# Delta-rule attention and hash-routed experts on one core: products of the experts in one of five widths, chosen by a branch of TensorE

## The chip, the core and the metric

One core of a Trainium2 chip runs the whole kernel. The metric is the device time of one execution in microseconds (us); less is better. The engines are named as in the profile: PE (TensorE: matmuls, with PEld for its weight loads), DVE (VectorE), ACT (ScalarE), POOL (GpSimd) and SP (SyncE). Each engine has a sequencer of its own that reads the engine's instructions in order.

## What is computed

The reference runs a delta-rule attention and hands its output, row by row, to a layer of eight experts:

```
# q, k, v: (4, 8, 768, 48), beta: (4, 8, 768)
k_n = k / (|k| + 1e-6)
for t in range(768):                       # per batch and head, state (48, 48)
    y[t]  = q[t] @ state
    state = state + beta[t] * outer(k_n[t], v[t] - state.T @ k_n[t])
x = y as rows (batch, t) of all heads: (3072, 384)
expert = token_ids * 2654435761 % 8        # the low three bits of the id
for e in range(8):
    rows      = x[expert == e]
    out[rows] = relu(rows @ w1[e]) @ w2[e] # w1: (8, 384, 1024), w2: (8, 1024, 384)
```

All numbers are float32. How many rows an expert gets depends on the token ids. With the inputs given here the eight experts get 364, 389, 385, 423, 360, 376, 420 and 355 of the 3072 rows.

## The kernel before

The kernel has two parts. The first (to line 827, the first 270 us or so) is the attention: time is cut into 24 chunks of 32 steps, the states stay in PSUM, and a list written out by hand orders the work of all engines (the schedule is manual: each engine executes its instructions in the order in which the program issues them). It leaves its rows in a scratch tensor in DRAM, `x_scratch`. In its last chunks, `routing()` works out on DVE, from the token ids, a table of slots: `gx` holds for each slot the row of `x_scratch` to fetch, `gidx` the row of the output to write. `routing()` is cut into steps by `yield`; the number behind a `yield` is the time that a small planner (`Work`) reckons for the step, and the chunk loop takes as many steps as it has time for.

Each expert has room for `CAP` = 424 rows, as `KT` = 4 tiles of `TS` = 106 rows. Rows beyond that go to an overflow loop at the end (line 937 on), which runs no time with these inputs. For expert 0 alone, the first three tiles (`KE`) are fetched before the attention has ended, and so hold only rows of its first 21 chunks (`CE`); `shift` moves the ranks of the later rows up so that they begin in the fourth tile. The kernel before does that for all eight experts.

The second part runs the experts one after the other. For expert e the loop has four steps:

- gemm1 (line 851): for each of the 8 blocks `fo` of 128 hidden units, 3 matmuls of 128x128 weights by 128x424 rows into one of two PSUM banks, by turns; after an even block ACT, after an odd one DVE applies the relu and copies to `h_sb`.
- rows of the expert before out (`put_all`, lines 872 to 877): for each of 4 tiles, 3 transposes by PE, a copy to `o_sb` by DVE or ACT, and an indirect DMA by POOL that scatters 112 rows.
- rows of the next expert in (`turn_one`, lines 843 and 845): for each of 4 tiles, 3 transposes by PE and a copy to `xT` by DVE.
- gemm2 (line 864): for each of the 3 blocks `co` of 128 outputs, 8 matmuls into one of two banks, then a copy to `yT` by ACT or DVE (line 866).

A float32 matmul is two records in the profile, each with a weight load of its own, so each product of an expert has 48 records of PE and 48 of PEld. Weights sit in three sets of buffers. SP issues the loads of expert e + 3 (`load_w`, lines 83 and 86) behind gemm2 of expert e; POOL issues the gathers of expert e + 2's rows behind gemm1 of expert e.

Of the kernel before, what the change touches and what calls it, by code (L numbers as in the profile page):

```python
# [9 lines left out]
F32 = mybir.dt.float32  # L10
BF16 = mybir.dt.bfloat16
I32 = mybir.dt.int32
ACT = mybir.ActivationFunctionType
ALU = mybir.AluOpType
# [5 lines left out]
def kernel(  # L20
# [11 lines left out]
    nc = tc.nc  # L32
    P = 128
    B, H, S, D = q.shape
    N, DIN = out.shape
    E, _, F = moe_w1.shape
    C = 32
    CO = DIN // P
    FO = F // P
    NTC = N // P  # L40
# [2 lines left out]

    KT = 4
    KE = 3
    TS = 106
    TD = 112
    CAP = KT * TS  # L50
    CE = 21
    NOV = -(-(N - CAP) // P)
    NHI = E * KT + NOV
    BIG = 1 << 20


    x_dram = nc.dram_tensor("x_scratch", (N, DIN), F32, kind="Internal").ap()
# [8 lines left out]
    gidx = keep.tile([P, NHI], I32)  # L66
    gx = keep.tile([P, NHI], I32)
    ov_i = keep.tile([P, NOV + 1], I32)


    wts = ctx.enter_context(tc.tile_pool(name="wts", bufs=1))
# [39 lines left out]
    def bank(pool, tag):  # L111
        return pool.tile([P, BANK], F32, tag=tag, name="ps" + tag.upper())

    ctx.enter_context(tc.manual_schedule())
    with ExitStack() as phase1:
# [101 lines left out]
        def routing():  # L217

            V = nc.vector
# [10 lines left out]
            for b in range(B):  # L230
# [57 lines left out]
            V.tensor_tensor(sums, incl_f, sums, op=ALU.subtract)  # L288
            V.tensor_tensor(rank_f, rank_f, sums, op=ALU.add)

            yield 0.7
            shift = rt.tile([P, E], F32)
            V.tensor_scalar(out=shift, in0=incl[:, :, CE - 1], scalar1=-1.0,
                            scalar2=float(KE * TS), op0=ALU.mult, op1=ALU.add)
            V.tensor_scalar(out=shift, in0=shift, scalar1=0.0, scalar2=None, op0=ALU.max)
            V.tensor_tensor(rank[:, :, CE:], rank[:, :, CE:],
                            shift[:, :, None].to_broadcast([P, E, NTC - CE]), op=ALU.add)

            yield 0.9
            V.tensor_tensor(shift, shift, incl[:, :, NTC - 1], op=ALU.add)  # L300
            more = rt.tile([P, E, NTC], F32)
            V.tensor_tensor(more, shift[:, :, None].to_broadcast([P, E, NTC]),
                            thr[:, None, :].to_broadcast([P, E, NTC]), op=ALU.is_gt)
            blocks = rt.tile([P, E], F32)
            V.tensor_reduce(blocks, more, axis=AX.X, op=ALU.add)
# [523 lines left out]
    with tc.tile_pool(name="m_xg", bufs=8) as m_xg, \  # L829
         tc.tile_pool(name="m_h", bufs=2) as m_h, \  # L830
         tc.tile_pool(name="m_y", bufs=1) as m_y, \
         tc.tile_pool(name="m_o", bufs=5) as m_o:

        xTs = [t[:, :CO * CAP].rearrange("p (c n) -> p c n", c=CO) for t in XTs]

        yTs = [m_y.tile([P, CO, CAP + TD - TS], F32, name=f"yT{i}") for i in range(2)]
        for t in yTs:
            nc.vector.memset(t[:, :, CAP:], 0.0)

        def turn(xg, xT, col, width):  # L840
            xT_ps = bank(ps_t, "t")[:, :CO * P].rearrange("p (c n) -> p c n", c=CO)
            for co in range(CO):
                nc.tensor.transpose(xT_ps[:, co, :width], xg[:width, co * P:(co + 1) * P],
                                    ident[:width, :width])
            nc.vector.tensor_copy(xT[:, :, col:col + width], xT_ps[:, :, :width])  # L845

        def gemm1(i, xT, h_sb, cols):
            for fo in range(FO):
                h_ps = bank(*((ps_k, "k"), (ps_w, "w"))[fo % 2])
                for co in range(CO):  # L850
                    nc.tensor.matmul(h_ps[:, cols], lhsT=W1s[i][:, co, fo * P:(fo + 1) * P],  # L851
                                     rhs=xT[:, co, cols], start=(co == 0), stop=(co == CO - 1))
                if fo % 2 == 0:
                    nc.scalar.activation(h_sb[:, fo, cols], h_ps[:, cols], ACT.Relu)  # L854
                else:
                    nc.vector.tensor_scalar(out=h_sb[:, fo, cols], in0=h_ps[:, cols], scalar1=0.0,  # L856
                                            scalar2=None, op0=ALU.max)

        def gemm2(i, h_sb, yT, width):

            for co in range(CO):
                y_ps = bank(ps_s, f"s{co % 2}")
                for fo in range(FO):
                    nc.tensor.matmul(y_ps[:, :width], lhsT=W2w[i][:, fo, co * P:(co + 1) * P],  # L864
                                     rhs=h_sb[:, fo, :width], start=(fo == 0), stop=(fo == FO - 1))
                (nc.vector.tensor_copy if co % 2 else nc.scalar.copy)(yT[:, co, :width],  # L866
                                                                      y_ps[:, :width])

        def put(yT, col, width, idx, kt, alone):
            o_ps = bank(*((ps_g, "g"), (ps_y, "y"))[kt % 2])  # L870
            for co in range(CO):
                nc.tensor.transpose(o_ps[:width, co * P:(co + 1) * P], yT[:, co, col:col + width],
                                    ident)
            o_sb = m_o.tile([P, DIN], F32, name="o_sb")
            (nc.scalar.copy if kt % 2 else nc.vector.tensor_copy)(o_sb[:width],  # L875
                                                                  o_ps[:width, :DIN])
            scat = nc.gpsimd.indirect_dma_start(  # L877
                out=out[:, :], out_offset=bass.IndirectOffsetOnAxis(ap=idx[:width], axis=0),
                in_=o_sb[:width], in_offset=None, bounds_check=N - 1, oob_is_err=False)
            if alone:  # L880
                tc.declare_no_dep(scat.ins, group="scatters", reason="disjoint rows")
                tc.add_to_no_dep_group("scatters", scat.ins)

        xgs = {(0, kt): xg0[kt] for kt in range(KT)}

        def fetch(e):
            for kt in range(KT):
                xgs[e, kt] = m_xg.tile([P, DIN], F32, name="xg")
                gather(x_dram, gx[:, e * KT + kt:e * KT + kt + 1], xgs[e, kt])

        def turn_one(e, kt):
            turn(xgs.pop((e, kt)), xTs[e % 3], kt * TS, TS)

        def put_all(e):
            for kt in range(KT):
                put(yTs[e % 2], kt * TS, TD, gidx[:, e * KT + kt:e * KT + kt + 1], kt, True)

        def new_h():
            return m_h.tile([P, FO, CAP], F32, name="h_sb")


        gather(x_dram, gx[:, KE:KT], xg0[KE])
        for kt in range(KE):
            turn_one(0, kt)
        for _ in load_w(1, nc.gpsimd):
            pass

        for i in range(8):
            nc.vector.memset(m_xg.tile([P, DIN], F32, name="xg"), 0.0)
        fetch(1)  # L910
        for _ in load_w(2, nc.gpsimd):
            pass
        for e in range(E):
            h_sb = new_h()
            if e == 0:
                gemm1(0, xTs[0], h_sb, slice(0, KE * TS))
                turn_one(0, KE)
                gemm1(0, xTs[0], h_sb, slice(KE * TS, CAP))
            else:
                gemm1(e % 3, xTs[e % 3], h_sb, slice(0, CAP))  # L920
            if e + 2 < E:
                fetch(e + 2)
            if e > 0:

                put_all(e - 1)
            if e + 1 < E:
                for kt in range(KT):
                    turn_one(e + 1, kt)
            gemm2(e % 3, h_sb, yTs[e % 2], CAP)
            if e + 3 < E:  # L930
                for _ in load_w(e + 3, nc.sync):
                    pass
        put_all(E - 1)


        n_ov = nc.values_load(ov_i[0:1, NOV:NOV + 1], min_val=0, max_val=NOV)
        with tc.For_i(0, n_ov, 1) as it:
            ex = nc.values_load(ov_i[0:1, bass.ds(it, 1)], engines=[mybir.EngineType.Pool],
                                min_val=0, max_val=E - 1)
            for _ in load_w(None, nc.gpsimd, 0, ex):  # L940
                pass
            idx = m_o.tile([P, 1], I32, name="idx")
            nc.vector.tensor_copy(idx, gidx[:, bass.ds(it + E * KT, 1)])
            idx_x = m_o.tile([P, 1], I32, name="idx_x")
            nc.vector.tensor_copy(idx_x, gx[:, bass.ds(it + E * KT, 1)])
            xg = m_xg.tile([P, DIN], F32, name="xg")
            nc.vector.memset(xg, 0.0)
            nc.gpsimd.indirect_dma_start(
                out=xg, out_offset=None, in_=x_dram[:, :],
                in_offset=bass.IndirectOffsetOnAxis(ap=idx_x[:, 0:1], axis=0),  # L950
                bounds_check=N - 1, oob_is_err=False)
            turn(xg, xTs[0], 0, P)
            h_sb = new_h()
            gemm1(0, xTs[0], h_sb, slice(0, P))
            gemm2(0, h_sb, yTs[0], P)
            put(yTs[0], 0, P, idx[:, 0:1], 0, False)


# [26 lines left out]
```

## Time and profile before

| what | us |
|---|---|
| three runs | 595.12, 595.18, 597.61 |
| median | 595.18 |
| the profiled execution | 593.35 |
| its span, from the first to the last instruction | 591.8 |
| PE busy / weight loads busy | 527.1 / 377.6 |
| DVE / ACT / POOL busy | 271.0 / 197.5 / 255.2 |
| mean clock granted to PE | 0.944 |

The time of an execution is its span and some 1.5 us around it. Matmuls are pipelined, and their ends are modelled: the mean duration of one matmul (519 ns) overlaps the next, and the distance from start to start is read from the busy time of many. Weight loads overlap matmuls. "Issue" as the releaser of a wait means that the profile shows nothing that the engine waited for. A sequencer's own instructions (register moves, branches, waits that stand alone) are not on the page; where they are spoken of below, they are read from the trace's raw records, as is the start of a single instruction fetch. Times of such records are given from the start of the span, too.

### The profile page before, as it was taken

How to read it: one execution, taken by the hardware profiler on the slowest of the kernel's cores; microseconds unless marked ns; L12 is line 12 of the kernel's file. 1: busy time of each engine (PE TensorE's matmuls, PEld its weight loads, DVE VectorE, ACT ScalarE, POOL GpSimd, SP SyncE). 2: the span in 40 equal slices, each digit the busy share in tenths (PEclk: the TensorE clock that was granted, in tenths of full speed). 3: DMA queues.
4: the chain of work that ended last, by engine and by line, in shares of the span. 5: the costliest groups of instructions: out<-in, count | busy, mean ns of one | idle time of the engine just before them, and what ended most of it. 6: DMA issues, size and time to landing. Idle time of an engine off the chain costs nothing. (4 is left out here: it accounts for less than half of the span.)

```text
span 591.8 us, 13888 instructions
## 1 busy us (share of the span) xinstructions
PE 527.1 (89%) x5548; PEld 377.6 (64%) x5548; DVE 271.0 (46%) x717; ACT 197.5 (33%) x429; POOL 255.2 (43%) x409
## 2 busy tenths in 40 slices
PE   8968889889888577879899999999999999999991
PEld 7857878888888577766755555555555555555551
DVE  6899898989899875833210201212012030120100
ACT  5866677787786232421101111011010110110100
POOL 9509677787878764943830310503205010020112
PEclk9559899999999987986999999999999999999997
DMA  6927678698685754853973440434315300010011
GB/s 110 180 41 120 112 131 155 122 156 155 120 151 105 128 119 88 174 129 91 371 230 106 156 130 14 176 106 144 115 39 188 106 22 17 0 40 0 8 37 39
DMA packets 130242, 65.57 MB, mean 111 GB/s; under 512 B 112858, under 2 KB 120114, under 8 KB 130176
## 3 DMA queue, kind: packets, MB, share of 16 engines
q1 hardware_dynamic: 113328, 33.12, 27.1%
q0 software_dynamic: 15328, 28.39, 19.4%
q10 hardware_dynamic: 1520, 3.15, 1.8%
q8 instruction: 45, 0.74, 0.6%
q14 instruction: 21, 0.17, 0.1%
HBM read 49.67 MB, written 10.22 MB: 101 GB/s over the span
## 5 line engine op out<-in xcount | busy, mean ns | idle before, releaser
L864 PE MATMUL psS<-h_sb,w 128*128 128x424 f32 x384 | 138.1, 519 | 0.0
L877 POOL DMA_INDIRECT out_dram<-o_sb,gidx x32 | 30.4, 950 | 231.4 <-DVE o_sb L875 224.1
L864 PEld LDWEIGHTS psS<-h_sb,w 128*128 128x128 f32 x384 | 72.3, 190 | 61.0 <-issue 61.0
L856 DVE TENSOR_SCALAR h_sb<-psW 128x424 f32<-128x424 f32 (+2 forms) x36 | 19.8, 550 | 157.8 <-PE psW L851 155.1
L851 PE MATMUL psK<-xT,w 128*128 128x424 f32 (+2 forms) x216 | 76.5, 491 | 1.4 <-DVE xT L845 1.4
L851 PE MATMUL psW<-xT,w 128*128 128x424 f32 (+2 forms) x216 | 74.8, 482 | 0.0
L172 POOL DMA_DIRECT2D K<-in_k_dram x96 | 55.4, 583 | 42.6 <-PE psS L606 36.2
L517 DVE TENSOR_TENSOR U<-U,tmp 128x31 f32<-128x31 f32 (+15 forms) x186 | 63.8, 343 | 6.4
L515 DVE TENSOR_TENSOR tmp<-U,Ni 128x31 f32<-128x31 f32 (+15 forms) x186 | 63.3, 340 | 5.3
L851 PEld LDWEIGHTS psK<-xT,w 128*128 128x128 f32 x216 | 40.2, 194 | 31.9 <-issue 29.4
L851 PEld LDWEIGHTS psW<-xT,w 128*128 128x128 f32 x216 | 39.6, 191 | 29.9 <-issue 28.2
L551 POOL DMA_DIRECT2D MB<-MT x96 | 55.3, 583 | 4.5 <-PE psG L617 2.0
L178 POOL DMA_DIRECT2D V<-in_v_dram x96 | 55.3, 583 | 4.0 <-DMA V<-in_v_dram 1.3
L866 ACT COPY yT<-psS 128x424 f32<-128x424 f32 x16 | 8.2, 512 | 143.3 <-PE psS L864 115.2
L854 ACT ACTIVATE h_sb<-psK 128x424 f32<-128x424 f32 (+2 forms) x36 | 17.4, 484 | 110.3 <-PE psK L851 109.2
L452 PE MATMUL psG<-sd,w 96*64 96x64 f32 x640 | 30.0, 243 | 17.1 <-ACT sd L431 11.7
L594 PE MATMUL psW<-R,TB 128*64 128x48 f32 x736 | 33.6, 230 | 12.6 <-DVE R L579 8.3
L866 DVE COPY yT<-psS 128x424 f32<-128x424 f32 x8 | 4.8, 601 | 87.1 <-PE psS L864 87.1
L600 ACT ACTIVATE W<-psW 64x192 f32<-64x192 f32 x96 | 31.1, 324 | 39.7 <-PE psW L594 34.2
L606 PE MATMUL psS<-W,K 128*96 128x96 f32 x368 | 42.2, 260 | 1.6 <-ACT W L600 1.6
L439 ACT ACTIVATE w<-psT,own 96x512 f32<-96x512 f32 x66 | 43.2, 688 | 0.4
L606 PEld LDWEIGHTS psS<-W,K 128*96 128x96 f32 x368 | 37.4, 172 | 3.3 <-ACT W L600 1.9
(186 smaller groups left out, 696.7 us busy)
## 6 DMA issues: line engine op xcount, KB each, us to landing
w<-in_moe_w_dram SPq DMA_DIRECT2D x15, 512.0 KB
w<-in_moe_w_dram SPq DMA_DIRECT2D x20, 384.0 KB
Kd<-in_k_dram SPq DMA_DIRECT2D x24, 192.0 KB
Qd<-in_q_dram SPq DMA_DIRECT2D x24, 192.0 KB
K<-in_k_dram POOLq DMA_DIRECT2D x96, 48.0 KB
V<-in_v_dram POOLq DMA_DIRECT2D x96, 48.0 KB
x_scratch<-x_sb SPq DMA_DIRECT2D x96, 48.0 KB
TB<-TU SPq DMA_DIRECT2D x96, 32.0 KB
```

Source lines behind the costliest of these rows:

```text
L172: nc.gpsimd.dma_start(out=K4s[c % 3][quarter(i), :, i % 2, :], in_=k_r[i, c * C:(c + 1) * C])
L178: nc.gpsimd.dma_start(out=Vs[c][quarter(i)], in_=v_r[i, c * C:(c + 1) * C])
L439: nc.scalar.activation(to[:, :, :, r], psT, ACT.Copy, scale=own[:, r:r + 1])
L515: V.tensor_tensor(tmp, U[:, j:j + 1, 0:n].to_broadcast([P, m, n]), Ni[:, j, j + 1:, None].to_broadcast([P, m, n]), op=ALU.mult)
L517: V.tensor_tensor(U[:, j + 1:, 0:n], U[:, j + 1:, 0:n], tmp, op=ALU.add)
L551: eng.dma_start(out=dst[quarter(i), :, i, :], in_=src[quarter(i)])
L594: nc.tensor.matmul(psW[pair(p), i], lhsT=TBs[c % 2][:, HT * h + i, 2 * p:2 * p + 2].rearrange("k r t -> k (r t)"), rhs=Rs[h][:, i], start= ...
L600: nc.scalar.activation(Ws[h][pair(p), :, p], psW[pair(p)], ACT.Copy)
L606: nc.tensor.matmul(psS[h][:, i], lhsT=K4s[c % 3][:, HT * h + i], rhs=Ws[h][:, i], start=(c == 0 and i == 0), stop=True, skip_group_check=True)
L851: nc.tensor.matmul(h_ps[:, cols], lhsT=W1s[i][:, co, fo * P:(fo + 1) * P], rhs=xT[:, co, cols], start=(co == 0), stop=(co == CO - 1))
L864: nc.tensor.matmul(y_ps[:, :width], lhsT=W2w[i][:, fo, co * P:(co + 1) * P], rhs=h_sb[:, fo, :width], start=(fo == 0), stop=(fo == FO - 1))
L877: scat = nc.gpsimd.indirect_dma_start(out=out[:, :], out_offset=bass.IndirectOffsetOnAxis(ap=idx[:width], axis=0), in_=o_sb[:width], in_of ...
```

## The change

The routing also counts, for each expert, which of five widths holds its rows: 360, 376, 392, 408 or 424 (`WIDTHS`, from 0 to 4), and stores that number in `wid_i`. The ranks are shifted for expert 0 only. With these inputs the rows used are 375 (364 and a shift of 11), 389, 385, 423, 360, 376, 420 and 355, so the widths are 376, 392, 392, 424, 360, 376, 424 and 360.

PE's sequencer loads the number into a register (`arm`), and every group of matmuls is written five times, once per width, as the five bodies of a switch that only PE takes part in. A gemm1 group is now a pair of blocks `fo` (6 matmuls, 12 records of PE and 12 of PEld), a gemm2 group one block `co` (8 matmuls, 16 and 16 records). The switch is a jump through a register: two register moves and a product give the distance, each body starts at the beginning of a 16 KB block of instructions, holds at its top a hint that names the block behind the switch, and ends in a jump to it. Four PSUM banks instead of two serve each product, and both copies of a pair come after the pair. ACT and DVE copy all 424 columns as before. Expert 0's gemm1 has fixed widths (318, then 106 columns) and no switch; its gemm2 has one.

Between the products, the tiles of rows out and rows in alternate (out 0, in 0, out 1, in 1 and so on), and the copies of the rows in alternate between ACT and DVE.

```diff
+    WIDTHS = [CAP - 16 * i for i in range(4, -1, -1)]
...
+    wid_i = keep.tile([P, E], I32)
...
-            yield 0.7
-            shift = rt.tile([P, E], F32)
-            V.tensor_scalar(out=shift, in0=incl[:, :, CE - 1], scalar1=-1.0,
+            yield 0.9
+            shift = rt.tile([P, 1], F32)
+            V.tensor_scalar(out=shift, in0=incl[:, 0, CE - 1:CE], scalar1=-1.0,
                             scalar2=float(KE * TS), op0=ALU.mult, op1=ALU.add)
             V.tensor_scalar(out=shift, in0=shift, scalar1=0.0, scalar2=None, op0=ALU.max)
-            V.tensor_tensor(rank[:, :, CE:], rank[:, :, CE:],
-                            shift[:, :, None].to_broadcast([P, E, NTC - CE]), op=ALU.add)
-
-            yield 0.9
-            V.tensor_tensor(shift, shift, incl[:, :, NTC - 1], op=ALU.add)
+            V.tensor_scalar(out=rank[:, 0, CE:], in0=rank[:, 0, CE:], scalar1=shift[:, 0:1],
+                            scalar2=None, op0=ALU.add)
+            used = rt.tile([P, E], F32)
+            V.tensor_copy(used, incl[:, :, NTC - 1])
+            V.tensor_tensor(used[:, 0:1], used[:, 0:1], shift, op=ALU.add)
+
+            yield 1.0
+            wid = rt.tile([P, E], F32)
+            V.tensor_scalar(out=wid, in0=used, scalar1=float(WIDTHS[0]), scalar2=None,
+                            op0=ALU.is_gt)
+            for n in WIDTHS[1:-1]:
+                V.scalar_tensor_tensor(out=wid, in0=used, scalar=float(n), in1=wid, op0=ALU.is_gt,
+                                       op1=ALU.add)
+            V.tensor_copy(wid_i, wid)
+
+            yield 0.7
...
-        def turn(xg, xT, col, width):
+        def copy(eng, out, in_):
+            (nc.scalar.copy if eng is nc.scalar else nc.vector.tensor_copy)(out, in_)
+
+        def turn(xg, xT, col, width, eng):
...
-            nc.vector.tensor_copy(xT[:, :, col:col + width], xT_ps[:, :, :width])
+            copy(eng, xT[:, :, col:col + width], xT_ps[:, :, :width])
...
+        banks = [bank(*t) for t in ((ps_k, "k"), (ps_w, "w"), (ps_s, "s0"), (ps_s, "s1"))]
+
+        def widths(arm):
+
+            if isinstance(arm, int):
+                yield arm
+            else:
+                for i in tc.Switch({mybir.EngineType.PE: arm}, len(WIDTHS)):
+                    yield WIDTHS[i]
+
+        def gemm1(i, xT, h_sb, arm, lo=0, hi=CAP):
+
+            for f in range(0, FO, 2):
+                h_ps = banks[f // 2 % 2 * 2:][:2]
+                for width in widths(arm):
+                    for fo in range(2):
+                        for co in range(CO):
+                            nc.tensor.matmul(
+                                h_ps[fo][:, lo:width],
+                                lhsT=W1s[i][:, co, (f + fo) * P:(f + fo + 1) * P],
+                                rhs=xT[:, co, lo:width], start=(co == 0), stop=(co == CO - 1))
+                nc.scalar.activation(h_sb[:, f, lo:hi], h_ps[0][:, lo:hi], ACT.Relu)
+                nc.vector.tensor_scalar(out=h_sb[:, f + 1, lo:hi], in0=h_ps[1][:, lo:hi],
+                                        scalar1=0.0, scalar2=None, op0=ALU.max)
+
+        def gemm2(i, h_sb, yT, arm, hi=CAP):
 
             for co in range(CO):
...
+                y_ps = banks[co]
+                for width in widths(arm):
+                    for fo in range(FO):
+                        nc.tensor.matmul(y_ps[:, :width],
+                                         lhsT=W2w[i][:, fo, co * P:(co + 1) * P],
+                                         rhs=h_sb[:, fo, :width], start=(fo == 0),
+                                         stop=(fo == FO - 1))
+                copy((nc.scalar, nc.vector)[co % 2], yT[:, co, :hi], y_ps[:, :hi])
...
         def turn_one(e, kt):
-            turn(xgs.pop((e, kt)), xTs[e % 3], kt * TS, TS)
...
+            turn(xgs.pop((e, kt)), xTs[e % 3], kt * TS, TS, (nc.scalar, nc.vector)[kt % 2])
+
+        def put_one(e, kt):
+            put(yTs[e % 2], kt * TS, TD, gidx[:, e * KT + kt:e * KT + kt + 1], kt, True,
+                (nc.vector, nc.scalar)[kt % 2])
+
+        def arm(e):
+            return nc.values_load(wid_i[0:1, e:e + 1], engines=[mybir.EngineType.PE], min_val=0,
+                                  max_val=len(WIDTHS) - 1)
...
+        arms = {}
         for e in range(E):
             h_sb = new_h()
             if e == 0:
-                gemm1(0, xTs[0], h_sb, slice(0, KE * TS))
+                gemm1(0, xTs[0], h_sb, KE * TS, 0, KE * TS)
+                arms[0] = arm(0)
                 turn_one(0, KE)
-                gemm1(0, xTs[0], h_sb, slice(KE * TS, CAP))
+                gemm1(0, xTs[0], h_sb, CAP, KE * TS)
             else:
-                gemm1(e % 3, xTs[e % 3], h_sb, slice(0, CAP))
+                gemm1(e % 3, xTs[e % 3], h_sb, arms[e])
+            if e + 1 < E:
+                arms[e + 1] = arm(e + 1)
             if e + 2 < E:
                 fetch(e + 2)
-            if e > 0:
-
-                put_all(e - 1)
-            if e + 1 < E:
-                for kt in range(KT):
+
+            for kt in range(KT):
+                if e > 0:
+                    put_one(e - 1, kt)
+                if e + 1 < E:
                     turn_one(e + 1, kt)
-            gemm2(e % 3, h_sb, yTs[e % 2], CAP)
+            gemm2(e % 3, h_sb, yTs[e % 2], arms[e])
```

More of the change, by code (lines that the diff above doesn't have):

```diff
@@ L289, in routing @@
             V.tensor_tensor(rank_f, rank_f, sums, op=ALU.add)
-            yield 0.7
-            shift = rt.tile([P, E], F32)
-            V.tensor_scalar(out=shift, in0=incl[:, :, CE - 1], scalar1=-1.0,
+            yield 0.9
+            shift = rt.tile([P, 1], F32)
+            V.tensor_scalar(out=shift, in0=incl[:, 0, CE - 1:CE], scalar1=-1.0,
                             scalar2=float(KE * TS), op0=ALU.mult, op1=ALU.add)
             V.tensor_scalar(out=shift, in0=shift, scalar1=0.0, scalar2=None, op0=ALU.max)
-            V.tensor_tensor(rank[:, :, CE:], rank[:, :, CE:],
-                            shift[:, :, None].to_broadcast([P, E, NTC - CE]), op=ALU.add)
-            yield 0.9
-            V.tensor_tensor(shift, shift, incl[:, :, NTC - 1], op=ALU.add)
+            V.tensor_scalar(out=rank[:, 0, CE:], in0=rank[:, 0, CE:], scalar1=shift[:, 0:1],
[12 more added lines that the diff above has]
+            yield 0.7
             more = rt.tile([P, E, NTC], F32)
-            V.tensor_tensor(more, shift[:, :, None].to_broadcast([P, E, NTC]),
+            V.tensor_tensor(more, used[:, :, None].to_broadcast([P, E, NTC]),
                             thr[:, None, :].to_broadcast([P, E, NTC]), op=ALU.is_gt)
@@ L844, in turn @@
                                     ident[:width, :width])
[L845 to L857, printed above, removed]
@@ L859, in gemm2 @@
-        def gemm2(i, h_sb, yT, width):
-            for co in range(CO):
[L862 to L867, printed above, removed]
@@ L869, in put @@
-        def put(yT, col, width, idx, kt, alone):
+            copy(eng, xT[:, :, col:col + width], xT_ps[:, :, :width])
[19 more added lines that the diff above has]
+                                        scalar1=0.0, scalar2=None, op0=ALU.max)
@@ L870, in put @@
+        def put(yT, col, width, idx, kt, alone, eng):
             o_ps = bank(*((ps_g, "g"), (ps_y, "y"))[kt % 2])
@@ L874, in put @@
             o_sb = m_o.tile([P, DIN], F32, name="o_sb")
-            (nc.scalar.copy if kt % 2 else nc.vector.tensor_copy)(o_sb[:width],
-                                                                  o_ps[:width, :DIN])
+            copy(eng, o_sb[:width], o_ps[:width, :DIN])
             scat = nc.gpsimd.indirect_dma_start(
@@ L891, in turn_one @@
         def turn_one(e, kt):
-            turn(xgs.pop((e, kt)), xTs[e % 3], kt * TS, TS)
-        def put_all(e):
-            for kt in range(KT):
-                put(yTs[e % 2], kt * TS, TD, gidx[:, e * KT + kt:e * KT + kt + 1], kt, True)
+            turn(xgs.pop((e, kt)), xTs[e % 3], kt * TS, TS, (nc.scalar, nc.vector)[kt % 2])
[5 more added lines that the diff above has]
+                                  max_val=len(WIDTHS) - 1)
         def new_h():
@@ L915 @@
             if e == 0:
-                gemm1(0, xTs[0], h_sb, slice(0, KE * TS))
+                gemm1(0, xTs[0], h_sb, KE * TS, 0, KE * TS)
+                arms[0] = arm(0)
                 turn_one(0, KE)
-                gemm1(0, xTs[0], h_sb, slice(KE * TS, CAP))
+                gemm1(0, xTs[0], h_sb, CAP, KE * TS)
             else:
-                gemm1(e % 3, xTs[e % 3], h_sb, slice(0, CAP))
+                gemm1(e % 3, xTs[e % 3], h_sb, arms[e])
+            if e + 1 < E:
+                arms[e + 1] = arm(e + 1)
             if e + 2 < E:
                 fetch(e + 2)
-            if e > 0:
-                put_all(e - 1)
-            if e + 1 < E:
-                for kt in range(KT):
+            for kt in range(KT):
+                if e > 0:
+                    put_one(e - 1, kt)
+                if e + 1 < E:
                     turn_one(e + 1, kt)
-            gemm2(e % 3, h_sb, yTs[e % 2], CAP)
+            gemm2(e % 3, h_sb, yTs[e % 2], arms[e])
             if e + 3 < E:
@@ L932 @@
                     pass
-        put_all(E - 1)
+        for kt in range(KT):
+            put_one(E - 1, kt)
         n_ov = nc.values_load(ov_i[0:1, NOV:NOV + 1], min_val=0, max_val=NOV)
@@ L951 @@
                 bounds_check=N - 1, oob_is_err=False)
-            turn(xg, xTs[0], 0, P)
+            turn(xg, xTs[0], 0, P, nc.vector)
             h_sb = new_h()
-            gemm1(0, xTs[0], h_sb, slice(0, P))
-            gemm2(0, h_sb, yTs[0], P)
-            put(yTs[0], 0, P, idx[:, 0:1], 0, False)
+            gemm1(0, xTs[0], h_sb, P, 0, P)
+            gemm2(0, h_sb, yTs[0], P, P)
+            put(yTs[0], 0, P, idx[:, 0:1], 0, False, nc.vector)
 _INS = ['q', 'k', 'v', 'beta', 'moe_token_ids', 'moe_w1', 'moe_w2']
```

## The prediction

> **What bounds the kernel now.** I read the page first (engines, slices, costliest groups), then PE's waits and busy time by stretch for the experts' part, then PE's timeline of one expert, last the DMA view of the tail. The chain of waits holds only the last 2 us and says nothing here.
>
> ```profile
> span 591.8 us, 13888 instructions
> PE 527.1 (89%) x5548; PEld 377.6 (64%) x5548; DVE 271.0 (46%) x717; ACT 197.5 (33%) x429; POOL 255.2 (43%) x409
> q8 instruction: 45, 0.74, 0.6%
> L864 PE MATMUL psS<-h_sb,w 128*128 128x424 f32 x384 | 138.1, 519 | 0.0
> ```
>
> PE is the busiest engine; DVE and ACT are slack in the second half. The third line (packets, MB, share of 16 engines) is TensorE's own instruction stream: 45 fetches of 16 KB [...]. So a block is fetched as the stream gets there; nothing is held far ahead.
>
> ```profile
> 490.00:520.80 30.80, 30.80 (x88) 16.39 (x87) 2.40 (x4) 3.12 (x6) 0.00 (x0) 1.00 0.00 1
> 520.80:524.64 3.84, 3.03 (x25) 2.42 (x24) 2.68 (x6) 0.96 (x2) 1.87 (x2) 1.00 0.13 42
> 524.64:541.70 17.06, 17.06 (x50) 9.15 (x49) 1.30 (x3) 0.51 (x1) 1.88 (x2) 1.00 0.08 25
> ```
>
> Columns: stretch, length, busy us of PE, PEld, DVE, ACT, POOL, then PE's clock. In the products PE is busy all the time at full clock; DVE and ACT are idle nine tenths of it. Only between the products (520.80 to 524.64) does PE have gaps.
>
> ```profile
> 486.69 17.26 PE L864 MATMUL psS<-h_sb,w 128*128 128x424 f32 x48
> 503.79 2.30 PE L851 MATMUL psK<-xT,w 128*128 128x424 f32 x6
> 505.93 2.30 PE L851 MATMUL psW<-xT,w 128*128 128x424 f32 x6
> ...
> 520.87 0.49 PE L872 MATMUL psG<-ident,yT 128*112 128x128 f32 x3
> 521.20 0.49 PE L872 MATMUL psY<-ident,yT 128*112 128x128 f32 x3
> 522.19 0.54 PE L872 MATMUL psG<-ident,yT 128*112 128x128 f32 x3 [0.50 <-DVE o_sb L875]
> ...
> 523.92 0.89 PE L843 MATMUL psT<-ident,xg 106*128 106x106 f32 x6 [0.31 <-DVE xT L845]
> 524.64 17.26 PE L864 MATMUL psS<-h_sb,w 128*128 128x424 f32 x48
> ```
>
> One expert is 524.64 - 486.69 = 37.95 us: gemm2 17.10, gemm1 17.08, rows out and in 3.77. Each product has 48 records, so 17.1/48 = 0.356 us each, 0.84 ns per column: time goes with the width. Weights wait for nobody in this part: no wait of PE on a DMA is listed.
>
> ```profile
> PE psG L872 <- DVE o_sb L875: 3.8, 8, 0.5
> PE psT L843 <- DVE xT L845: 1.9, 6, 0.3
> ```
>
> [...] no branch into a cold block is on the path before. [...] PE's two compare-and-branches in the tail took 101 and 304 ns. [...] its wait on expert 6's W1, an instruction of the sequencer's own, stands at 497.41 in the raw records, 6.4 us (18 matmuls) ahead of gemm1 at 503.79.
>
> **Part 1, narrower products (gain).** The chosen widths are 376, 392, 392, 424, 360, 376, 424, 360. Columns saved against 8 x 424: 288 in gemm2; in gemm1 240, since expert 0 keeps its fixed widths. At 48 records and 0.833 ns (0.356 us less some 3 ns, over 424): gemm2 288 x 48 x 0.833 = 11.5 us, gemm1 240 x 48 x 0.833 = 9.6. Together -21.1. Weight loads (190 ns) stay under the shortest matmul (360 x 0.833 = 300 ns). ACT and DVE still copy all 424 columns, 0.5 to 0.6 us per copy, under products of 3.6 us and more; four banks instead of two cover them. Without that cover each would cost its 0.6 us.
>
> **Part 2, interleaving and alternating engines (gain).** It takes away the waits above: in experts 1 to 7 about 7 x 0.5 + 6 x 0.31 = 5.4 us, of which expert 7 (rows out only) keeps 0.5: -4.9. What is late next is the PE's own transposes, 24 records. The number and the order of POOL's scatters per expert stay; they go on as copies land, under gemm2.
>
> **Part 3, the switches (cost).** 7 experts x 4 + 8 x 3 = 52 switches. Each is a computed jump to one of five bodies, each at the start of its own block, then a jump out to the block behind the fifth. So TensorE's sequencer needs two cold blocks per switch [...]. A fetch was: in the tail, the taken branch ends at 581.29 and the next block's transfer begins at 582.14 (0.85 us later) and takes 1.02 us; the 45 average 0.006 x 16 x 591.8/45 = 1.26. Lowest bound 0.85 + 0.90 (shortest record) = 1.75; [...] I take the middle, F = 2.4. Beside it: set-up of two moves and a product of registers (87 ns from one such instruction to the next in the tail) and the jump (304 ns), 0.57; a hint, 0.09; the jump out, 0.30. The hint asks for the exit block at the top of the body, but issuing 24 to 32 matmuls and loads takes under 0.5 us (12 in at most 0.25 us in the last rows out), so the exit fetch is exposed to the sequencer almost whole. One switch holds the sequencer T = 0.57 + 2.4 + 0.09 + 2.4 + 0.30 = 5.76 us.
>
> What lies beside it is the array's work of the arm before: a gemm1 arm has 12 matmuls, 3.64 us at 360 to 4.28 at 424 (27.53 over experts 1 to 7); a gemm2 arm 16, 4.85 to 5.70 (41.77 over all eight). The excess is idle PE:
> - gemm1, gaps between four arms: 3 x (7 x 5.76 - 27.53) = 38.4.
> - gemm2, gaps between three: 2 x (8 x 5.76 - 41.77) = 8.6.
> - into gemm1, behind the last gemm2 arm (36.92 for experts 0 to 6): 7 x 5.76 - 36.92 = 3.4.
> - into gemm2: the sequencer is held by the waits of the transposes until shortly before (0.5 us of lead), so set-up + F + 0.2 of refill - 0.5 = 2.67, x 8 = 21.4.
>
> Queued behind the jump is all of PE's stream, and ACT and DVE's relus, copies, and so POOL's scatters wait with it. Sum +71.8.
>
> **Part 4, the rest.** PE loads 8 arm numbers (one register load in the tail: 484 ns) behind gemm1's last arm; sequencer then has about 0.57 + 2.7 + 0.6 us beside 3.6 to 4.3 of array: 0, and at worst 8 x 0.5 = 4. VectorE gets six more small operations in routing; the nearest row (128x8, 274 ns) bounds them at 1.6; VectorE is busy 10.92 of 15 us there: 0.8 taken. SP's weight loads are issued later as PE is, but have a whole expert of slack.
>
> Sum: -21.1 - 4.9 + 71.8 + 0.8 = +46.6 on the profiled execution's 593.35, 640.0. The median shown is 1.8 higher (595.18): 642. With F at its ends, T is 4.46 or 7.16: gaps 27 or 139, so 597 to 709 in the same terms.
>
> **Rivals.**
> - The exit is covered (faster). If the exit block is in place when the arm has been issued, a switch holds the sequencer 0.57 + 2.4 + 0.5 + 0.3 = 3.8 us, under nearly all arms; only the 21.4 into gemm2 is left: -26.0 + 21.4 + 0.8, 591. For it: the hint is asked at the top. Against: a 0.5 us body ahead of a 2.4 us fetch. The point from which it decides is T = 4.4.
> - Jumps are nearly free: all five bodies already there. Then -26 + 3 + 0.8: 573. Against: 45 fetches, one per block.
> - Fetches queue behind the in-order prefetch. The tail shows that a jump triggers the fetch of the following block; if that goes first, the exit waits 1.1 and the arm 0.5 us more: T = 7.4, gaps 148, 718.
> - PE is drained at each join: at the tail's skipped loop PE waits for its own counter before branching. 52 x (0.57 + 2.4 + 0.2) = 165, less 25: 735. Against: all five arms count alike, so nothing is to be made even.
>
> **Chances.** Forecast 0.50, exit covered 0.15, free 0.08, queued 0.17, drained 0.10. Under 0.5% is about what a measurement of this kernel can tell from no change. Faster 0.20 (most of covered, and free), same 0.06 (the rest of covered, and the forecast's low end), slower 0.74. The range 588 to 716 takes in covered, the forecast from end to end and nearly reaches queued; free, drained and about half of queued are left out.
>
> **What would show it.** In the changed profile: matmul means fall with width; some 104 more instruction fetches on q8 (two per switch); PE idle with "issue" as its releaser, 1.8 us between gemm1 arms and 2.7 ahead of gemm2; next to none between gemm2 arms at 424; the waits for o_sb and xT gone. It is wrong if those gaps are under 0.3 us (jumps cheap), if the fetches don't rise, or if the gaps are as long between gemm2's arms as between gemm1's (a drain).

## The result and the profile after

The changed kernel takes 807.64 us (median of 4, 805.02 to 811.08) where the kernel before takes 595.15 (591.01 to 597.61): a ratio of 1.358, 95% interval 1.349 to 1.368. Slower was forecast, but 642 us, and the range ended at 716. The profiled execution took 811.08 us. Some executions of a kernel run a per cent or two longer than its others, at a lower granted clock (the kernel before on the chip of the first experiments: 596.37 us at 0.919 beside 584.38 at 0.950); the medians below take all executions, the ratios leave those out.

Two lines of the page of before (the span in 40 slices: PE's busy share and its granted clock, in tenths), then the lines of the changed kernel's page that answer to these and to those shown in the prediction:

```profile
PE   8968889889888577879899999999999999999991
PEclk9559899999999987986999999999999999999997
```

```profile
span 809.5 us, 14456 instructions
PE 587.2 (73%) x5548; PEld 408.8 (51%) x5548; DVE 265.0 (33%) x707; ACT 202.9 (25%) x445; POOL 255.3 (32%) x409
PE   7489899898778967656666677686765576587673
PEclk9798999999689687887877889788888788979797
q8 instruction: 218, 3.57, 2.5%
```

The work is the same number of records (5548), but PE is busy 73% of a longer span. In the experts' part, where PE's digits were 9 before but for the last, they now lie between 5 and 8 (from the fifteenth slice on, but for the last), and the granted clock between 0.7 and 0.9. Instruction fetches go from 45 to 218.

PE's timeline from expert 4's gemm2 into expert 5's gemm1 (start, length, line, what it works on, count, idle time before it and what ended that):

```profile
582.25 5.10 PE L896 MATMUL psK<-h_sb,w 128*128 128x360 f32 x16
592.44 6.57 PE L896 MATMUL psW<-h_sb,w 128*128 128x360 f32 x16 [5.09 <-issue]
601.02 6.79 PE L896 MATMUL psS<-h_sb,w 128*128 128x360 f32 x16 [2.00 <-issue]
612.19 3.79 PE L882 MATMUL psK<-xT,w 128*128 128x376 f32 x6 [4.38 <-issue]
615.77 2.14 PE L882 MATMUL psW<-xT,w 128*128 128x376 f32 x6
622.06 5.74 PE L882 MATMUL psS<-xT,w 128*128 128x376 f32 x12 [4.15 <-issue]
631.71 2.88 PE L882 MATMUL psK<-xT,w 128*128 128x376 f32 x6 [3.91 <-issue]
```

Ahead of each group of a switch but the first of these, PE stands still for 2 to 5 us, and the releaser is "issue": no engine and no DMA of data was waited for. From group to group it is 9 to 11 us, where 3.8 to 4.9 us of work (at full clock) lie in a group. PE's waits in the experts' part, in total, times and longest:

```profile
PE psS L882 <- issue: 49.4, 14, 5.1
PE psK L882 <- issue: 42.5, 13, 6.2
PE psK L896 <- issue: 28.8, 7, 6.5
PE psW L896 <- issue: 22.6, 7, 5.2
PE psS L896 <- issue: 19.2, 8, 4.6
PE psG L905 <- DVE o_sb L855: 0.8, 2, 0.5
```

The waits for `o_sb` and `xT` are all but gone, as forecast; 162 us of "issue" have come. The trace's raw records hold the sequencer's own instructions, and here the time is: each switch has two branch records, a jump into a body and a jump out of it, and nearly all of them last microseconds. Sorted by the number of fetches that began during the branch or within 0.8 us before it:

```
jump in,  1 fetch : 18, median 2.89 us (2.62 to 6.54), together  64.3
jump in,  2 fetches: 32, median 4.55 us (4.38 to 6.24), together 151.5
jump out, 1 fetch : 14, median 2.92 us (2.75 to 3.33), together  41.2
jump out, 2 fetches: 38, median 4.66 us (4.41 to 7.68), together 185.0
two more jumps in  : 0.39 and 1.03 us, no fetch
```

These are 443 us. The two jumps without a fetch lead into gemm2 of experts 4 and 7, which take the first body, the block behind the one that holds the jump; the first of them stands at 581.64, and in the timeline the group behind it starts without a wait. From the first jump in at 296.84 us to the end of the last jump out at 795.57 are 498.7 us; the rest are some 0.24 us between a jump in and its jump out, 0.33 us from there to the next jump, and 3 to 5 us per expert for the rows. So in this stretch the sequencer hardly waited for the array; it set the time.

### The profile page after: what moved, and what is told of

Its sections match the earlier page's. It is cut to its first block, busy times and chain, and to the rows that moved or that the text cites. A ratio compares the mean times of both kernels' runs of the same rounds, so it can differ in the third digit from the quotient of the medians.

```text
span 809.5 us, 14456 instructions
## 1 busy us (share of the span) xinstructions
PE 587.2 (73%) x5548; PEld 408.8 (51%) x5548; DVE 265.0 (33%) x707; ACT 202.9 (25%) x445; POOL 255.3 (32%) x409
## 5 line engine op out<-in xcount | busy, mean ns | idle before, releaser
L882 PE MATMUL psS<-xT,w 128*128 128x392 f32 (+5 forms) x216 | 91.0, 584 | 49.4 <-issue 49.4
L882 PEld LDWEIGHTS psS<-xT,w 128*128 128x128 f32 x216 | 49.4, 244 | 90.6 <-issue 83.6
L882 PE MATMUL psK<-xT,w 128*128 128x392 f32 (+5 forms) x108 | 51.5, 629 | 43.8 <-issue 42.5
L896 PE MATMUL psK<-h_sb,w 128*128 128x424 f32 (+3 forms) x128 | 57.4, 614 | 28.9 <-issue 28.8
L896 PE MATMUL psW<-h_sb,w 128*128 128x424 f32 (+3 forms) x128 | 52.8, 575 | 22.6 <-issue 22.6
L896 PE MATMUL psS<-h_sb,w 128*128 128x424 f32 (+3 forms) x128 | 52.0, 568 | 19.2 <-issue 19.2
L882 PEld LDWEIGHTS psK<-xT,w 128*128 128x128 f32 x108 | 24.3, 245 | 66.6 <-issue 63.1
L896 PEld LDWEIGHTS psK<-h_sb,w 128*128 128x128 f32 x128 | 30.2, 243 | 52.8 <-issue 45.8
L896 PEld LDWEIGHTS psW<-h_sb,w 128*128 128x128 f32 x128 | 28.4, 227 | 47.0 <-issue 39.9
L896 PEld LDWEIGHTS psS<-h_sb,w 128*128 128x128 f32 x128 | 27.6, 221 | 43.6 <-issue 35.9
```

Of the source, the lines that this page charges most:

```text
L882: nc.tensor.matmul(h_ps[fo][:, lo:width], lhsT=W1s[i][:, co, (f + fo) * P:(f + fo + 1) * P], rhs=xT[:, co, lo:width], start=(co == 0), sto ...
```

## The experiments

Theory A: the loss is the sequencer's jumps into blocks of instructions that aren't there; width and interleaving gain about what was reckoned. Rivals: B, the new grouping costs time itself; C, PE is drained at each branch or join, a fixed price that nothing covers; D, the clock, which falls to half in spells; E, for the hint, that it does nothing.

**Without any switch.** Two runs, the first with each expert's width as a constant, the second 424 for all:

```diff
-            return nc.values_load(wid_i[0:1, e:e + 1], engines=[mybir.EngineType.PE], min_val=0,
-                                  max_val=len(WIDTHS) - 1)
+            return (376, 392, 392, 424, 360, 376, 424, 360)[e]     # second run: return CAP
```

> The changed kernel with the eight widths written into the program (376, 392, 392, 424, 360, 376, 424, 360), so without any switch; it holds only for these inputs. Theory A (the loss is the switches' jumps into cold blocks of instructions; narrower products and interleaving gain what was reckoned): 593.35 - 21.1 - 4.9 + 0.8, about 568 us. Rival B (pairs in four banks, copies after the pair, or the interleaving cost time themselves): 590 us or more.

> The changed kernel with every product 424 wide and no switch: only pairs, banks, interleaving, alternating copies and the routing are left of the change. Theory A: the waits between the products go, 593.35 - 4.9 + 0.8, about 589 us. Rival B: 595 us or more.

Measured: 556.93 us, ratio 0.953 (0.947 to 0.959), and 578.94 us, ratio 0.991 (0.986 to 0.996). The kernel before took 586.58 us on this chip, so ratios compare better than times: A had 0.957 (568 / 593.35) and 0.993 (589 / 593.35), B 0.994 and 1.003 at least, and B falls. The experts' part, from the start of expert 0's first gemm1 to the start of PE's last matmul, compares best. It is 307.3 us before, 297.4 with all of the change but widths and switches, 276.3 with the widths too, and 525.5 in the changed kernel, so the whole loss lies there. Width gains 297.4 - 276.3 = 21.1. Of the step before it, 307.3 - 297.4 = 9.9, 1.6 us are not the interleaving's: expert 0's first gemm1 took 14.56 us in the trace of before, at half clock for its first 3.3 us, and 12.94 here, at full clock. The interleaving's are 8.3, all in the turns of the rows. PE's timeline of the second run, rows out and in:

```profile
506.75 0.49 PE L905 MATMUL psG<-ident,yT 128*112 128x128 f32 x3
507.08 0.44 PE L860 MATMUL psT<-ident,xg 106*128 106x106 f32 x3
...
509.05 0.44 PE L860 MATMUL psT<-ident,xg 106*128 106x106 f32 x3
509.32 5.88 PE L896 MATMUL psK<-h_sb,w 128*128 128x424 f32 x16
```

509.32 - 506.75 = 2.57 us where the kernel before needed 3.77, 1.2 us less in each of experts 1 to 6, though the waits listed there were only 0.5 + 0.31. Expert 0's turn of the rows went from 2.74 to 1.62; that of expert 7 (2.02) stayed.

Against the run with constants, the changed kernel's experts' part is 249 us longer. Some 162 of them are idle time of PE; over 80 are the same matmuls drawn out (PE busy 337.5 us from 297 us on, 254.0 with constants from 288 on), at a clock of 0.83 in place of 1.00. Whether the clock costs time of its own is rival D.

**A chain of compare-and-branches in place of the computed jump.** The five bodies then lie one behind the other, 24 or 32 instructions of matmuls and loads each:

```diff
-                for i in tc.Switch({mybir.EngineType.PE: arm}, len(WIDTHS)):
-                    yield WIDTHS[i]
+                with ExitStack() as elses:
+                    for i in range(len(WIDTHS)):
+                        if i == len(WIDTHS) - 1:
+                            yield WIDTHS[i]
+                        else:
+                            with tc.If(arm == i) as cmp:
+                                yield WIDTHS[i]
+                            elses.enter_context(cmp.Else())
```

> The changed kernel with the switch replaced by a chain of four compare-and-branches; the five bodies lie one behind the other in the stream, 24 or 32 matmuls and loads each, not each at the start of a block. Theory A: no jump goes further than about 130 instructions, into a block that is there or on its way; up to four branches of 0.1 to 0.3 us per group hide under 3.6 to 5.7 us of matmuls: 568 to 585 us. Rival C (any branch of TensorE empties its queue or waits for the array): 52 times 3 us and more, over 700 us.

> The chain of compare-and-branches again, in five rounds beside the kernel before: a ratio of 0.95 to 0.96, some 3 us above the widths written into the program.

> The chain of compare-and-branches as a tree of depth two to three, the bodies still one behind the other. Theory A: all branches lie under the matmuls but for those into gemm2, so within 2 us of the chain: a ratio of 0.95 to 0.96 to the kernel before. Rival C: as the chain had it, nothing above 0.97.

Measured: 562.81 us, ratio 0.954 (0.947 to 0.961); again, in five rounds, 562.44 us, 0.956 (0.950 to 0.963); as a tree 567.02 us, 0.952 (0.943 to 0.961). A's 568 to 585 us are ratios of 0.957 to 0.986. PE's timeline and waits of the second of these runs, the same place between expert 4's products:

```profile
424.66 3.79 PE L888 MATMUL psS<-xT,w 128*128 128x360 f32 x12
428.29 0.49 PE L911 MATMUL psG<-ident,yT 128*112 128x128 f32 x3
...
430.86 5.02 PE L902 MATMUL psK<-h_sb,w 128*128 128x360 f32 x16
435.72 4.70 PE L902 MATMUL psW<-h_sb,w 128*128 128x360 f32 x15
```

```profile
PE psK L902 <- issue: 1.0, 2, 0.5
PE psG L911 <- DVE o_sb L855: 0.8, 2, 0.5
PE psK L888 <- DVE xT L855: 0.8, 1, 0.8
```

The same choice of width by a branch of PE, the same groups and joins, and "issue" is down to 1.0 us. Its 173 branch records have a median of 0.21 us, 170 of them under 0.5 us, 37.7 us in all, and all but 1.3 us of that lies under matmuls; 69 fetches stand against 218. The experts' part is 278.1 us, 1.8 above the constants. So these branches didn't drain PE, and C falls for branches. The chain changes two things at once, the form of the branch and the place of the bodies. The form alone isn't what costs: the changed kernel's own jumps through a register took 0.39 and 1.03 us where no fetch was needed. A computed jump among bodies that lie close together was not run. Both forms of the chain beat both kernels, and they choose at run time as the changed kernel does.

**One body always taken.** All five bodies 424 wide, and the arm number fixed at 2, 0 or 4:

```diff
-    WIDTHS = [CAP - 16 * i for i in range(4, -1, -1)]
+    WIDTHS = [CAP] * 5
...
-            V.tensor_copy(wid_i, wid)
+            V.tensor_scalar(out=wid_i, in0=wid, scalar1=0.0, scalar2=2.0, op0=ALU.mult,
+                            op1=ALU.add)
```

> The changed kernel with all five bodies 424 wide and the third body always taken, so that only the switch is tested. Theory A, with the in-order prefetch going first: every jump in and every jump out takes the long form (medians 4.55 and 4.66 us in the changed kernel, where 18 jumps in and 14 jumps out were short, 2.9 us); the sequencer sets the time and the wider products cost nothing: 811 + 18 x 1.65 + 14 x 1.75, about 865 us. Rival C (waits for the array at the joins): the 21 us of wider products, and no more, 832 us.

> As the run with the third body, but always the first body: it lies next behind the block that holds the jump. Theory A with the in-order prefetch going first: the jump in needs one fetch, and that one is on its way already (2.9 us instead of 4.6), the jump out stays long: 856 - 52 x 1.65, about 770 us. Rival C (the length of a jump has nothing to do with the place of its target): 856 us.

> As the run with the third body, but always the fifth body: the block behind the switch is next behind it. Theory A with the in-order prefetch going first: the jump in stays long, the jump out is short (2.9 instead of 4.65 us): 856 - 52 x 1.75, about 766 us, with two thirds of the fetches per jump out. Rival C: 856 us.

Measured, in one execution each: 856.55, 763.16 and 781.38 us. The instruction fetches of the three (packets, MB, share):

```profile
q8 instruction: 246, 4.03, 2.9%
```

```profile
q8 instruction: 195, 3.19, 2.4%
```

```profile
q8 instruction: 194, 3.18, 2.1%
```

The same work, and up to 93 us between places of the target. The median jump in is 4.7, 3.0 and 4.7 us, the median jump out 4.8, 4.9 and 3.2: short where the target is the next block in order (the first body behind the jump, the exit block behind the fifth body), long elsewhere. The totals of single executions also hold what happens ahead of the experts: their part begins at 266.9 us in the first of these runs and at 279.2 in the changed kernel on this chip. By the experts' part alone the changed kernel has 527.5 us here, the three runs 576.7, 481.8 and 501.6: 49 more, 46 and 26 less. A had 54 more, and from there 86 and 91 less (measured: 95 and 75); C had 21 more for the first (832 - 811), and no difference between the three.

One thing goes against the part of A by which the fetch of the block next in order goes first and so makes a jump long. A jump into gemm2 comes 2.1 to 5.5 us after the jump out before it, and in the changed kernel six of the eight show one fetch only; they last no less, 3.9 to 6.5 us, since the fetch begins 1.0 to 3.9 us into the jump. Why it begins so late no run shows.

**The clock.** Four more products of 424 columns ahead of each jump in, their result unread; and the changed kernel again on the same chip:

```diff
+                pad = bank(ps_g, "g")
+                for _ in range(4):
+                    nc.tensor.matmul(pad[:, :CAP], lhsT=ident, rhs=W1s[0][:, 0, :CAP],
+                                     start=True, stop=True)
                 for i in tc.Switch({mybir.EngineType.PE: arm}, len(WIDTHS)):
```

> The changed kernel with four more products of 424 columns (8 records, 2.9 us at full clock), whose result nobody reads, ahead of each of the 52 jumps in. Theory A (the sequencer alone sets the time, the array's clock and work lie beside its stalls): no change beyond 1%, with PE's granted clock higher. Rival D (the halved clock in the experts' part costs time of its own): faster by some 10 us and more. Rival C (PE is waited for at each jump): slower by 52 x 2.9, 150 us.

> The changed kernel itself, to stand beside the three others on the same chip: 800 to 811 us by either theory.

Measured, in one execution each: 818.5 us with the extra products, 818.88 without. That is 8 us above the upper end expected, though the kernel before was faster on this chip; against the first trace of the changed kernel, 5.7 of the 8 us lie ahead of the experts' part. Spans and clocks, with the extra products and without:

```profile
core 0: 816.9 us, clock 0.941
```

```profile
core 0: 817.3 us, clock 0.843
```

Without them the clock falls to half for 3.4 or 6.8 us at a time in the raw records; with them its mean (0.941) is where it was before the change (0.944), and nothing is gained: the experts' part is 534.0 against 527.5 us. 416 more matmul records disappear in the stalls. D falls, and C once more, which had 150 us for them. In the first trace of the changed kernel the falls go with idle stretches of PE: in the 3.4 us ahead of every fall in the experts' part PE was busy 0.51 of the time at most, ahead of every rise 0.88 of it and more. But the sequencer was later than even the slow array.

**Fewer switches.** The three groups of gemm2 in one switch:

```diff
-            for co in range(CO):
-                y_ps = banks[co]
-                for width in widths(arm):
+            for width in widths(arm):
+                for co in range(CO):
                     for fo in range(FO):
...
+            for co in range(CO):
+                copy((nc.scalar, nc.vector)[co % 2], yT[:, co, :hi], banks[co][:, :hi])
```

> The changed kernel with all three groups of gemm2 in one switch (36 switches instead of 52), its three copies behind it. Theory A: where the array has 14 to 17 us of work, the jump out and the next jump in (9.5 us together) are covered; an expert is then 3 x 9.4 + 3.9 for gemm1, 2.6 for the rows, 4.9 for the jump into gemm2 and 15.7 for gemm2, 55 us instead of some 67: about 730 us, with no gap ahead of gemm1's first group and one of 4 to 5 us ahead of gemm2. Rival C (a fixed price per switch that nothing covers, 818 - 568 over 52): 741 us, with a gap ahead of gemm1's first group like the others.

Measured, in one execution: 724.9 us. PE's timeline:

```profile
423.59 7.70 PE L895 MATMUL psK<-h_sb,w 128*128 128x392 f32 x16 [4.59 <-issue]
431.12 5.43 PE L895 MATMUL psW<-h_sb,w 128*128 128x392 f32 x16
436.39 5.43 PE L895 MATMUL psS<-h_sb,w 128*128 128x392 f32 x16
441.66 2.30 PE L882 MATMUL psK<-xT,w 128*128 128x424 f32 x6
443.79 2.30 PE L882 MATMUL psW<-xT,w 128*128 128x424 f32 x6
451.16 4.44 PE L882 MATMUL psS<-xT,w 128*128 128x424 f32 x6 [5.07 <-issue]
```

The gap ahead of gemm1's first group (441.66) is gone, the others stay, as A had it. And here all eight jumps out of gemm2 take 0.32 to 0.42 us: the hint at the top of the body is 9 to 14 us ahead of them. Two of the eight leave the fifth body, behind which their target comes next anyway; for the other six it is the hint that fits, though no run without it was made. In the changed kernel the hint is 0.15 to 0.32 us ahead, and the jumps out take 2.75 to 7.68 us. The kernel is still 1.22 times slower than the one before (592.44 us on this chip): the jumps in stay.

**A hint for the jump in.** Set ahead of the rows out and in:

```diff
+            hint = tc.switch_hint({mybir.EngineType.PE: arms[e]}, len(WIDTHS))
             for kt in range(KT):
...
-            gemm2(e % 3, h_sb, yTs[e % 2], arms[e])
+            gemm2(e % 3, h_sb, yTs[e % 2], arms[e], hint=hint)
```

> The changed kernel with a hint, set ahead of the rows out and in, that names the body of gemm2's first group (8 of the 52 jumps in). Theory A: the block is fetched beside the 2.6 us of transposes and the jump into gemm2 shrinks from some 4.6 us to under 2: 818 - 8 x 3, about 795 us. Rival E (a hint does nothing for a jump through a register): 818 us.

Measured, in one execution: 818.08 us, as E had it. The hint stands 2.4 to 4.2 us ahead of the eight jumps, and they take 32.0 us together, 30.9 in the changed kernel. Between the hint and the jump no fetch began in seven of the eight. Whether 4 us are too short for a hint or a hint of this kind isn't followed stays open; a longer lead wasn't tried.

## Why the prediction was wrong, step by step

- Bound and mechanism: right in the main. PE sets the end, a switch costs its sequencer fetches of cold blocks (218 fetches against 45), and "issue" is the name of PE's idle time in the profile. What the prediction had not foreseen is that a third of the loss (over 80 of 249 us) shows as slower matmuls and not as idle time; by the run with the extra products this cost nothing of its own. The arm numbers' loads cost next to nothing: the chain loads them too, and is 1.8 us above the constants in all.
- Part 1, width, -21.1: measured -21.1.
- Part 2, interleaving, -4.9: measured -8.3. The term was taken from the idle column, which starts at the modelled end of the last matmul; from start to start the turn of the rows became 1.2 us shorter in experts 1 to 6, 7.2 together, and not 0.8. Another 1.1 came in expert 0, whose two waits by "issue" (0.9 and 0.3 us) the term left out.
- Part 3, the step that failed, is the price of a jump to a cold block: "I take the middle, F = 2.4." The lower end, 1.75, came from the trace of before; the upper end, and so the middle, was the author's estimate, and no trace or run showed it. With the jump's own 0.30 that makes 2.7 us a jump; measured are 443 us over 104 jumps, 4.3 each. Where only one fetch ran and the target was next in order, 2.7 was near: 2.9. That is partly luck, for the transfer began some 0.45 us into the jump, not 0.85, and the jump went on for 1.4 us after the transfer's end, where F leaves 0.45 (2.4 - 0.85 - 1.1). But 70 of the 104 jumps had two fetches. The second began at 1.0 us and took 2.0 us beside the first, not 1.1, and the jump went on for 1.5 us after it: 4.6. The sum put this second fetch at nothing; only the rival "queued" had it, with 1.1 and 0.5 us. Two smaller points: the 45 fetches of before took 1.16 us on average by their records (1.26 came from a rounded share), and the 0.2 us of refill in the jumps into gemm2 was the author's estimate, which no trace shows.
- With all branches counted, T is (443 / 52) + 0.24 + 0.33 = 9.1 us in place of 5.76. Put into the prediction's own sum, it gives gaps of 3 x (63.7 - 27.5) + 2 x (72.8 - 41.8) + (63.7 - 36.9) + 8 x 4.3 = 232 us instead of 71.8, and 593 - 26 + 232 + 1 = 800 us; with the true gain of interleaving 797. Measured were 811; the 11 to 14 us left aren't assigned to any step.
- Part 4, 0.8 us for the routing's six operations: not to be told. Expert 0's first gemm1 begins at 273.45 instead of 273.00 us, but anywhere from 266.8 to 279.5 in the other runs.
- Fetches: in the trace of before the 45 fetches of 16384 bytes stand against 11282 records of PE, its weight loads and its sequencer, one for each 251. Some 104 more were forecast, 173 came. The counts fit a fetch of the block behind a target too, wherever it wasn't the next target itself: in the runs with one body, 3.9 fetches a switch with the third ((246 - 45) / 52), 2.9 with the first or the fifth.
- Rivals: by its number "drained" (735) came nearest, but it is refuted. By its mechanism it was "queued" (718): the place of the target counts as it had it, its price was too low, and its cause doesn't hold for the late single fetches into gemm2. "Exit covered" was right about the hint and wrong about the body's length. The clock was named by no rival.

The range was too narrow for what was known. Its upper end rested on an estimate that nothing measured bore out, for the trace of before has no jump into a cold block to measure.

## What to carry to other kernels

In these runs a branch of TensorE's sequencer was cheap (0.2 us, under a group of 3.6 us and more) when the five bodies lay one behind the other, some 120 to 160 instructions in all; a jump to a 16 KB block that was not there and not next in order cost 4 to 5 us, and twice that for in and out. So lay small alternatives close together behind compare-and-branches. The hint at the top of a body went with a short jump out (0.32 to 0.42 us) only where it stood 9 to 14 us ahead of it, and the jumps into those same bodies still took 1.3 to 6.2 us. When a resource isn't in the trace of before, such as a cold jump, let the range be as wide as ignorance of it; and measure gaps from start to start.

## What the runs showed of the hardware beyond that

Most jumps of PE's sequencer fell in three classes: 0.3 to 0.4 us without a fetch, 2.6 to 3.3 with one fetch, where the target was the block next in order, and 4.4 to 4.9 with two (up to 8.2; in both traces of the changed kernel the longest is the jump out of expert 0's first switch). No jump of the changed kernel that saw a fetch ended earlier than 1.34 us after the end of the last transfer. PE's clock fell to half and recovered again and again, some 35 times in the changed kernel's experts' part; where the extra products held it up (a mean of 0.941 in place of 0.843) nothing was gained, 534.0 us for that part in place of 527.5.
